# A SwiGLU block's last third by seven products for eight, with its sums made a block earlier

## The chip, the cores and the metric

One core of one Trainium2 chip runs the whole program. The metric is device time in microseconds of one execution, the median of several runs.

## The reference

```python
mask = q_bucket[:, :, :, None] == k_bucket[:, :, None, :]     # buckets: signs of 6 projections
scores = np.where(mask, scale * q @ k.T, -1e9)
attn = softmax(scores) @ v                                    # 4 batches, 8 heads, 768 rows, 64
x = attn.transpose(0, 2, 1, 3).reshape(3072, 512)
g = x @ w_gate                                                # w_gate, w_val: 512 x 1536
silu = g * (1.0 / (1.0 + np.exp(-g)))
out = (silu * (x @ w_val)) @ w_out                            # w_out: 1536 x 512
```

The change is in the second half, from `x` on.

## The kernel before

The attention comes first, a pair of heads at a time. Beside it the weights are read, rounded and split into 36 pieces, which are kept in DRAM (`ram`). `x` is kept transposed: its rows are the 512 features, 128 to a tile.

A product in fp32 is made of three matmuls. Every operand is kept as three parts, high, low and a difference (`[P, 3, 512]` per piece). The products of the first two parts go to one PSUM bank (tile `a`, 16 matmuls for 1024 tokens), those of the third to another (tile `n`, 8 matmuls). The result is `a * (STEP + 1) - n`: ScalarE reads `a` and scales it (L787), VectorE takes `n` off (L794).

The tokens are worked in three blocks of 1024 (the first, second and third block here; `NB` is 3). In each block there are 12 column blocks of 128 of the 1536 features, called U. A U takes one gate piece and one value piece: gate products, Silu (L796), value products, gate times value (L798), and the rounding of the hidden tile into its three parts (L799 on ScalarE, L805 low and L808 difference on VectorE). After three U's whose hidden tiles are ready comes a down part, D: eight chunks of 128 tokens, 9 matmuls each (tile `o`), added to the accumulators by VectorE (L851, L855; ScalarE's L849 in the first part). The last part of a block begins with four part chunks that leave out the last piece, and it stores the output on SP's queue.

The order is written out by hand: the scheduler is off, so every engine runs its instructions in the order in which the loop over `order` issues them. `atoms_of` yields the steps of a U (four: `a` and `n` of gate, `a` and `n` of value) and of a D (one per chunk), and after each of them the loop puts in some steps of other work. In the first block these are the remaining weight pieces (`turns`, paced by `pace`); in the second and third block there is nothing left of them. At a block's end the next block's `x` is loaded from DRAM into three `words` buffers (`load_x`) and split (`split_x`).

Pieces come into SBUF through a ring of six buffers (`bring`, L251, issued on POOL's queue): a load is issued when the piece six places before it has been used. PSUM's eight banks are four tiles of two banks (`two_banks`), taken in turn. All matmuls after the attention have line L748 (`mm`).

Of the kernel before, what the change touches and what calls it, by code (L numbers as in the profile page):

```python
# [8 lines left out]
FP32 = mybir.dt.float32  # L9
# [10 lines left out]
def kernel(  # L20
# [8 lines left out]
    moe_w_out: bass.AP,  # L29
    out: bass.AP,  # L30
):

# [6 lines left out]
    nc = tc.nc  # L41
# [33 lines left out]
    RINGS = (3, 3)  # L75
    ringp = [ctx.enter_context(tc.tile_pool(name="ringp", bufs=RINGS[0]))]
    dram = ctx.enter_context(tc.tile_pool(name="dram", bufs=1, space=bass.MemoryType.DRAM))
    pp = ctx.enter_context(tc.tile_pool(name="pp", bufs=4, space=PSUM))
    ctx.enter_context(tc.manual_schedule())

    def two_banks(name):
        return pp.tile([P, 2, 512], FP32, tag="pp", name=name)

    halves = [slice(half * HQ, (half + 1) * HQ) for half in range(2)]

# [138 lines left out]


    order = []
    for block in range(NB):
        for f in range(NF):
            order.append(("U", block * NF + f))
            if f % NQ == 0 and f:  # L230
                order.append(("D", (block * NF + f) // NQ - 1))
        order.append(("D", (block + 1) * NF // NQ - 1))
    wanted = []
    for kind, n in order:
        if kind == "U":
            wanted += [("g", n), ("v", n)]
        else:
            wanted += [("o", NQ * n + g) for g in range(NQ)]
    held = {}

    def bring(count=1):
        for _ in range(count):
            i = len(held)
            if i == len(wanted):
                return
            what, n = wanted[i]
            at = place[what, n % NF]
            assert progress["kept"] > at, (i, at, progress)
            pool = ringp[2 <= i % sum(RINGS) < 2 + RINGS[1]]
            held[what, n] = t = pool.tile([P, 3, PIECE], FP32R, tag="ring", name="ring")  # L250
            nc.gpsimd.dma_start(t.bitcast(FP32), ram[at].bitcast(FP32))  # L251

    kept_x = {(b, pr): dram.tile([P, S], FP32, tag=f"x{b}_{pr}", name="xram")
              for b in range(1, B) for pr in range(NP)}
# [481 lines left out]
    def gated_block(scope):  # L736
# [7 lines left out]
        rows = [out[b * S : (b + 1) * S, :].rearrange("(p c) m -> p c m", c=NCH) for b in range(B)]  # L744
        NCB = WB // P

        def mm(ps, w, x, start, stop):
            nc.tensor.matmul(ps, w, x, start=start, stop=stop)  # L748

        def up(F, what):  # L750
            b = F // NF
# [24 lines left out]
        def atoms_of(kind, n):  # L776
# [36 lines left out]
                    yield one  # L813
                    yield other
            else:
                b, part = divmod(n, NF // NQ)
                ws = [held["o", NQ * n + j] for j in range(NQ)]
                hs = [hids[NQ * n + j] for j in range(NQ)]
                tiles = {}

                def start(c, js, steps=None):
                    if c not in tiles:
                        tiles[c] = two_banks("o")
                    t = tiles[c]
                    cols = slice(c * P, (c + 1) * P)
                    def first():
                        for j in js:
                            for v in range(2):
                                mm(t[:, 0], hs[j][:, v, cols], ws[j][:, v],
                                   j == 0 and v == 0, j == NQ - 1 and v == 1)  # L830

                    def second():
                        for j in js:
                            mm(t[:, 1], hs[j][:, 2, cols], ws[j][:, 2], j == 0, j == NQ - 1)

                    for go in steps or ("ba" if final and c >= ahead else "ab"):
                        (first if go == "a" else second)()

                def end(c):
                    t = tiles.pop(c)  # L840
                    early = final and c >= ahead
                    if early:
                        nc.vector.tensor_tensor(accs[c], accs[c], t[:, 1], op=ALU.subtract)  # L843
                    if part == 0:
                        if c % 2 == 0:
                            accs[c // 2, "both"] = outp.tile([P, 2, DM], FP32, tag=f"o{c // 2}",
                                                             name="o")
                        accs[c] = accs[c // 2, "both"][:, c % 2]
                        nc.scalar.activation(accs[c], t[:, 0], AF.Copy, scale=STEP + 1)  # L849
                    else:  # L850
                        nc.vector.scalar_tensor_tensor(out=accs[c], in0=t[:, 0],  # L851
                                                       scalar=STEP + 1, in1=accs[c],
                                                       op0=ALU.mult, op1=ALU.add)
                    if not early:
                        nc.vector.tensor_tensor(accs[c], accs[c], t[:, 1], op=ALU.subtract)  # L855
                    if part == NF // NQ - 1:
                        batch, at = divmod(b * NCB + c, NCH)
                        if final and c >= ahead:
                            nc.sync.dma_start(rows[batch][:, at, :], accs[c])
                        elif c % 2:  # L860
                            nc.sync.dma_start(rows[batch][:, at - 1 : at + 1, :], accs[c // 2, "both"])
                    if c == NCB - 1:
                        bring(NQ)

                final = n == NB * NF // NQ - 1
                ahead = 4 if part == NF // NQ - 1 else 0
                for c in range(ahead):
                    yield lambda c=c: start(c, range(NQ - 1))
                def last_diffs(c):
                    tn = two_banks("o")[:, 0]  # L870
                    for j in range(NQ):
                        mm(tn, hs[j][:, 2, c * P : (c + 1) * P], ws[j][:, 2], j == 0, j == NQ - 1)
                    nc.vector.tensor_tensor(accs[c], accs[c], tn, op=ALU.subtract)

                def last(c):
# [3 lines left out]
                    for t, here, queue in ((ts[0], slice(0, DM - P), nc.sync),  # L879
                                           (ts[1], slice(DM - P, DM), nc.scalar)):  # L880
                        t = t[:, 0 : here.stop - here.start]
                        for j in range(NQ):
                            for v in range(2):
                                mm(t, hs[j][:, v, cols], ws[j][:, v, here],
                                   j == 0 and v == 0, j == NQ - 1 and v == 1)
                        nc.vector.scalar_tensor_tensor(out=accs[c][:, here], in0=t,  # L886
                                                       scalar=STEP + 1, in1=accs[c][:, here],
                                                       op0=ALU.mult, op1=ALU.add)
                        queue.dma_start(rows[batch][:, at, here], accs[c][:, here])

                for c in range(NCB):
# [5 lines left out]

                    def chunk(c=c):
                        if c >= ahead:
                            start(c, range(NQ))  # L900
                        else:
                            start(c, [NQ - 1], "ab")
                        end(c)
                    yield chunk

# [22 lines left out]

        raw_x = {}
        mine = turns()  # L930
        for kind, n in order:
            b, f = divmod(n, NF if kind == "U" else NF // NQ)
            changing = b + 1 < NB
            if changing:
                if (kind, f) == ("D", NF // NQ - 2):
                    load_x(b + 1, range(NP // 2))
                elif kind == "U" and f >= NF - 2:
                    assert len(added) == NPIECE
                    splits.extend(split_x(b + 1, f - NF + 2))
                    if f == NF - 1:  # L940
                        load_x(b + 1, range(NP // 2, NP))
            if n == NB * NF // NQ - 1 and kind == "D":
                finish(tails)
            for at, atom in enumerate(atoms_of(kind, n)):
                tail = atom()
                finish(tails)
                if tail:
                    tails.append(tail)
                if changing and kind == "U" and f >= NF - 2 and at:
                    splits.pop(0)()  # L950
                if changing and kind == "D" and f == NF // NQ - 1:
                    if at == 0:
                        more = [split_x(b + 1, pr) for pr in range(NP // 2, NP)]
                        for x in more:
                            x.pop(0)()
                    if at in (7, 10):
                        for x in more:
                            x.pop(0)()
                count[0] += 1
                if left and count[0] in (4, 6, 11):  # L960
                    left.append(left.pop(0)())
# [6 lines left out]
                    pace = (0, 0, 0, 2, 1, 2, 2, 2)  # L968
                else:
                    pace = (0, 0, 1, 0) + (1,) * 8  # L970
                for _ in range(pace[at]):
                    step = next(mine, None)
                    if step:
                        step()

    with ExitStack() as scope:
        gated_block(scope)
# [32 lines left out]
```

## Time and profile before

| | us |
|---|---|
| median of 3 runs | 907.73 (907.3 to 908.71) |
| the profiled execution, its own time | 908.05 |
| its span in the trace | 906.3 |
| TensorE busy (all matmuls) | 901.8 |
| VectorE, ScalarE, GpSimd busy | 665.4, 450.4, 90.6 |

The second block lies between 510.6 and 706.4 us of the span and the third between 706.4 and 902.5 us. Busy time of an engine is the time in which it executed something. TensorE's is close to the span, and its weight loads (PEld) run beside its matmuls. GpSimd (POOL) does little but issue the ring's loads in this half. Of the DMA traffic 114.8 MB go through POOL's queue (q0), and 57.4 MB through SP's (q1).

### The profile page before, as it was taken

Reading aid. Unit: us, or ns where it says so; the run is one execution under the profiler, and the core shown is the slowest. Engines: PE = TensorE matmul, PEld = TensorE weight load, DVE = VectorE, ACT = ScalarE, POOL = GpSimd, SP = SyncE. Lnnn points to the kernel's source line nnn. Section 1 sums busy time; section 2 is a strip of 40 time slices with the busy share of each in tenths; the row PEclk is TensorE's granted clock in tenths of the full one; section 3 lists DMA queues with packets and bytes.
Section 4 is the critical chain, followed back from the end, with each engine's and each line's share of the span. In section 5 each row is a group of like instructions: output and inputs, shape, how many; then the busy total and the mean of one; then the engine's idle time right before and its main releaser. Section 6 shows DMA issues by size and latency. Waiting matters only on the chain.

```text
span 906.3 us, 12438 instructions
## 1 busy us (share of the span) xinstructions
PE 901.8 (100%) x4801; PEld 638.4 (70%) x4801; DVE 665.4 (73%) x782; ACT 450.4 (50%) x604; POOL 90.6 (10%) x187
## 2 busy tenths in 40 slices
PE   9999999999999999999999999999999999999998
PEld 5444444444444588888888888888888888888887
DVE  6779999999988977688786856464658754474746
ACT  6788988788888654551524233331313243413220
POOL 2001100010001210011000000101000100001000
PEclk9999999999999999999999999999999999999999
DMA  7567888877877799685758563534434642525332
GB/s 181 109 145 183 190 203 194 205 203 230 229 195 213 225 358 375 240 294 170 300 173 296 193 249 105 180 134 172 142 140 150 250 149 98 200 70 209 104 140 93
DMA packets 142266, 174.24 MB, mean 192 GB/s; under 512 B 103200, under 2 KB 113408, under 8 KB 142208
## 3 DMA queue, kind: packets, MB, share of 16 engines
q0 software_dynamic: 22240, 114.83, 35.8%
q1 hardware_dynamic: 118560, 57.43, 24.5%
q10 hardware_dynamic: 1408, 1.20, 0.5%
q8 instruction: 38, 0.62, 0.3%
q14 instruction: 20, 0.16, 0.1%
HBM read 133.17 MB, written 39.42 MB: 190 GB/s over the span
## 4 chain that ended last, share of the span: by engine, by line
PE 99%; DVE 0%; DVEq 0%; issue 0%
PE a L748 29%; PE o L748 21%; PE sc L549 17%; PE n L748 14%; PE av L580 14%; PE joint L621 1%; PE joint L441 1%; PE idle L375 0%; PE tps L483 0%; DVE o L843 0%; DVE o L851 0%; DVE o L886 0%; DVEq L1005 0%; DVE kb L369 0%
## 5 line engine op out<-in xcount | busy, mean ns | idle before, releaser
L748 PE MATMUL a<-xparts,ring 128*128 128x512 f32 x1152 | 273.0, 389 | 0.0
L748 PEld LDWEIGHTS a<-xparts,ring 128*128 128x128 f32 x1152 | 216.2, 188 | 45.4 <-issue 0.6
L748 PE MATMUL o<-ring,hid 128*128 128x512 f32 (+1 forms) x870 | 198.2, 388 | 0.0
L748 PEld LDWEIGHTS o<-ring,hid 128*128 128x128 f32 x870 | 162.9, 188 | 33.6
L559 ACT ACTIVATE A<-sc 128x768 f32<-128x768 f32 x192 | 154.0, 815 | 1.6 <-PE sc L549 0.8
L549 PE MATMUL sc<-qT,kT 64*128 64x384 f32 x768 | 153.0, 483 | 0.0
L748 PE MATMUL n<-xparts,ring 128*128 128x512 f32 x576 | 142.2, 389 | 0.0
L580 PE MATMUL av<-A,vraw 128*64 128x386 f32 (+1 forms) x768 | 127.7, 488 | 0.0
L748 PEld LDWEIGHTS n<-xparts,ring 128*128 128x128 f32 x576 | 108.1, 188 | 22.4
L794 DVE TENSOR_TENSOR v<-v,n 128x1024 f32<-128x1024 f32 x36 | 44.0, 1221 | 97.5 <-PE n L748 97.0
L251 POOL DMA_DIRECT2D ring<-ram x108 | 57.0, 530 | 498.7 <-PE n L748 302.4
L580 PEld LDWEIGHTS av<-A,vraw 128*64 128x64 f32 x768 | 53.7, 136 | 73.3 <-issue 62.6
L787 ACT ACTIVATE g<-a 128x1024 f32<-128x1024 f32 x36 | 37.0, 1027 | 128.0 <-PE a L748 126.9
L549 PEld LDWEIGHTS sc<-qT,kT 64*128 64x128 f32 x768 | 68.8, 187 | 39.8 <-issue 35.3
L799 ACT ACTIVATE hid<-v 128x1024 fp32r<-128x1024 f32 x36 | 38.2, 1062 | 111.9 <-DVE v L798 108.2
L796 ACT ACTIVATE g<-g 128x1024 f32<-128x1024 f32 x36 | 38.2, 1061 | 87.9 <-DVE g L794 87.9
L855 DVE TENSOR_TENSOR o<-o 128x512 f32<-128x512 f32 x92 | 62.9, 687 | 19.0 <-ACT o L849 16.6
L794 DVE TENSOR_TENSOR g<-g,n 128x1024 f32<-128x1024 f32 x36 | 43.8, 1217 | 37.5 <-PE n L748 37.5
L549 PE MATMUL sc<-qb,kb 64*128 64x384 bf16 x384 | 63.5, 323 | 0.0
L603 DVE SCALAR_TENSOR_TENSOR both<-A 128x1536 f32<-128x1536 f32 x32 | 55.5, 1734 | 4.5 <-ACT A L559 3.0
L805 DVE SCALAR_TENSOR_TENSOR hid<-hid,v 128x1024 fp32r<-128x1024 f32 (+1 forms) x39 | 44.5, 1141 | 18.8 <-ACT hid L799 18.8
L607 DVE TENSOR_TENSOR both<-both,A 128x1536 f32<-128x1536 f32 x32 | 55.9, 1748 | 1.7
(88 smaller groups left out, 695.5 us busy)
## 6 DMA issues: line engine op xcount, KB each, us to landing
ring<-ram POOLq DMA_DIRECT2D x108, 768.0 KB, 5.6
ram<-stage POOLq DMA_DIRECT2D x22, 768.0 KB, 4.5
ram<-stage SPq DMA_DIRECT2D x14, 768.0 KB
vraw<-in_v_dram SPq DMA_DIRECT2D x16, 384.0 KB
kraw<-in_k_dram SPq DMA_DIRECT2D x60, 96.0 KB
qraw<-in_q_dram SPq DMA_DIRECT2D x60, 96.0 KB
r<-sums SPq DMA_DIRECT2D x28, 192.0 KB
out_dram<-o SPq DMA_DIRECT2D x10, 512.0 KB
```

The lines of the kernel that those rows point to most:

```text
L251: nc.gpsimd.dma_start(t.bitcast(FP32), ram[at].bitcast(FP32))
L549: nc.tensor.matmul(banks_of[u][:, h], x["k", n][rows, ks], x["q", n][rows, qs], start=start, stop=stop)
L559: nc.scalar.activation(weights(u)[:, :, 0:HQ], banks_of.pop(u), AF.Exp, scale=SCALE * (1.0 if units[u][0] else OFF / 2))
L580: nc.tensor.matmul(ps[h * D : (h + 1) * D, 0:width], raws["v", n][:, h, c, :], a[:, h, 0:width], start=c == 0, stop=c == NCH - 1)
L603: nc.vector.scalar_tensor_tensor(out=t, in0=first, scalar=S * EPS / P / 2, in1=now, op0=ALU.add, op1=ALU.add)
L607: nc.vector.tensor_tensor(t, t, now, op=ALU.add)
L748: nc.tensor.matmul(ps, w, x, start=start, stop=stop)
L794: nc.vector.tensor_tensor(two(z), two(z), n_, op=ALU.subtract)
L796: nc.scalar.activation(z, z, AF.Silu)
L799: nc.scalar.activation(h, val, AF.Copy, scale=TOWARD / STEP)
L805: nc.vector.scalar_tensor_tensor(out=l_, in0=h_.bitcast(FP32), scalar=-STEP, in1=v_, op0=ALU.mult, op1=ALU.add)
L855: nc.vector.tensor_tensor(accs[c], accs[c], t[:, 1], op=ALU.subtract)
```

## The change

In the third block two neighbouring column blocks of one weight, with the features cut in two halves of 256 and the tokens in two halves of 512, make a 2 x 2 by 2 x 2 product of quarters. It is done in seven products of quarters (6 matmuls each: two feature tiles, three parts) for eight. A group is such a set of seven: `g` or `v` for each of six pairs. With A the weights and B the tokens, the sums are S1 = A21 + A22, S2 = S1 - A11, S3 = A11 - A21, S4 = A12 - S2, and T1 = B12 - B11, T2 = B22 - T1, T3 = B22 - B12, T4 = B21 - T2.

Results that are used twice are copied: after A11 B11 ScalarE copies the two banks of Y to those of X, and A12 B21 is added to X by TensorE; after S2 T2 has been added to Y, Y is copied to Z; S3 T3 and then A22 T4 are added to Y, S4 B22 to Z. S1 T1 is read out to SBUF (`five`) and added by VectorE to two of the results. Each of the four results is read by ScalarE, and VectorE takes off the second bank (`less`). PSUM's tiles are single banks in this block. The rounding of the hidden tiles of one group is spread over the slots of the next group (`then`, `at_slot`).

The third block's down parts take four pieces for three, so there are three of them, with 12 matmuls per chunk. A group brings four ring pieces: the row, S1 and S2, S3 and S4, and the half of the second row that holds A22.

The sums are made in the second block, where `mine` is replaced by `all_sums`: 12 sets for the weights and 4 for x. Their steps are put in behind the steps of the U's and D's: two, one, two, one in a U, one per chunk in a D. A set loads two raw tiles into `words` buffers (SP), adds on GpSimd, rounds on ScalarE (`high`) and VectorE (`low`, `diff`) and stores to DRAM (SP). At the end of the second block T1 to T3 come back into the places of x's tiles and T4 into the three `words` buffers. B11, B21 and B22 are split from x as before, the last two earlier in the block's last D.

The order in which the engines get the work: TensorE has 3835 matmuls for 3905, VectorE 32 instructions on `made`, ScalarE 16, and POOL's queue now has the sets' additions among the ring's loads.

```diff
-    for block in range(NB):
+    for block in range(NB - 1):
...
+            else:
+                src = sums[what[0], n][:, 0 if what[1:] == "12" else 1]
...
+        def all_sums():
+            count = 2 * NG + 4
+            raws = {0: raw_parts(0)}
+            homes_ = {}
+            def add(i):
+                a, c = raws.pop(i)
+                t = homes_[i] = xparts_p.tile([P, 2, 3, PIECE], FP32, tag=f"x{2 + i % 2}", name="made")
+                tt = nc.gpsimd.tensor_tensor
+                lo, hi = slice(0, PIECE), slice(PIECE, 2 * PIECE)
+                if i < 2 * NG:
+                    tt(a[:, lo], a[:, lo], a[:, hi], op=ALU.add)
+                    tt(c[:, lo], c[:, lo], c[:, hi], op=ALU.add)
+                    k0, k1 = slice(0, HP), slice(HP, PIECE)
+                    s1, s2, s3, s4 = t[:, 0, 1, k0], t[:, 0, 1, k1], t[:, 1, 1, k0], t[:, 1, 1, k1]
+                    tt(s1, c[:, k0], c[:, k1], op=ALU.add)
+                    tt(s3, a[:, k0], c[:, k0], op=ALU.subtract)
+                    tt(s2, s1, a[:, k0], op=ALU.subtract)
+                    tt(s4, a[:, k1], s2, op=ALU.subtract)
...
+            def high(i):
+                t = homes_[i]
+                nc.scalar.activation(r32(t[:, :, 0]), t[:, :, 1], AF.Copy,
+                                     scale=TOWARD if i < 2 * NG else TOWARD / STEP)
...
+            for i in range(count + 1):
+                if i < count:
+                    yield lambda: add(i)
+                if i:
+                    yield lambda: low(i - 1)
+                    yield lambda: diff(i - 1)
+                if i + 1 < count:
+                    yield lambda: raws.update({i + 1: raw_parts(i + 1)})
+                if i < count:
+                    yield lambda: high(i)
...
-                    if at in (7, 10):
+                    if at in ((2, 4) if b == LAST - 1 else (7, 10)):
                         for x in more:
                             x.pop(0)()
+                        if at == 2:
+                            fourth_sum()
...
+                if b == LAST - 1:
+                    if kind == "U" and f < NF - 2 or kind == "D" and f < NF // NQ - 1:
+                        for _ in range((2, 1, 2, 1)[at] if kind == "U" else 1):
+                            step = next(made[0], None)
+                            if step:
+                                step()
+                    continue
...
+            product(Y, "A11", "B11", True, x_copy, lambda: copied(late["X"], Y, 1))
+            at_slot(1)
+            product(V, "S1", "T1", True, lambda: read(five, V), lambda: less(five, V))
+            at_slot(2)
+            product(Y, "S2", "T2", False, z_copy, lambda: copied(late["Z"], Y, 1))
+            bring()
+            at_slot(3)
+            X, Z = late["X"], late["Z"]
+            product(X, "A12", "B21", False, lambda: read(C[0, 0], X), lambda: less(C[0, 0], X))
+            bring()
+            if what == "v":
+                closing(0, 0)()
+            at_slot(4)
+            product(Y, "S3", "T3", False, lambda: read(C[1, 1], Y), lambda: less(C[1, 1], Y))
+            more_(C[1, 1])
+            if what == "g":
+                closing(0, 0)()
+            at_slot(5)
+            product(Z, "S4", "B22", False, lambda: read(C[0, 1], Z), lambda: less(C[0, 1], Z))
+            bring()
+            more_(C[0, 1])
+            closing(1, 1)()
+            at_slot(6)
+            product(Y, "A22", "T4", False, lambda: read(C[1, 0], Y), lambda: less(C[1, 0], Y))
+            bring()
+            if what == "g":
+                closing(0, 1)()
+                then(2, closing(1, 0))
+                return
...
+            then(1, closing(0, 1))
+            then(1, closing(1, 0))
+            then(1, lambda: high(0))
+            then(2, lambda: low(0))
+            then(3, lambda: diff(0))
+            then(3, lambda: high(1))
+            then(4, lambda: low(1))
+            then(5, lambda: diff(1))
```

`closing` is the Silu of a quarter (ScalarE) in a `g` group and gate times value (VectorE) in a `v` group; `more_` adds `five`; here `high`, `low` and `diff` at the end are those of the hidden tiles.

## Prediction, made blind

> **What bounds the kernel now.** I read the chain of work that ended last first, then its pieces in order of time, then the engines' busy time by block, then the DMA rate. The page's chain:
>
> ```profile
> PE 99%; DVE 0%; DVEq 0%; issue 0%
> PE a L748 29%; PE o L748 21%; PE sc L549 17%; PE n L748 14%; PE av L580 14%; PE joint L621 1%; PE joint L441 1%; PE idle L375 0%; PE tps L483 0%; DVE o L843 0%; DVE o L851 0%; DVE o L886 0%; DVEq L1005 0%; DVE kb L369 0%
> ```
>
> TensorE sets the end everywhere, so a matmul removed is worth its full pace, and any wait that PE doesn't have yet is a loss. The pace is in the chain in order of time (start, length, what), at the second block's first column block and first down part:
>
> ```profile
> 510.72 3.63 PE a L748 x16
> 514.35 1.81 PE n L748 x8
> ...
> 554.24 16.32 PE o L748 x72
> ```
>
> 3.63/16 and 16.32/72 are both 0.227 us per matmul (the 389 ns of the groups are overlapped durations). A column block U (two weights, 48 matmuls) is 10.88 us, a down part of 72 is 16.32 us, its chunk of 9 is 2.04 us. By block of 1024 tokens (PE, PEld, DVE, ACT, POOL busy, clock, DMA share, GB/s):
>
> ```profile
> 510.60:706.40 195.80, 195.80 (x866) 162.15 (x864) 118.74 (x127) 58.44 (x60) 18.93 (x36) 1.00 0.46 167
> 706.40:902.50 196.10, 196.10 (x871) 162.66 (x869) 114.30 (x125) 54.74 (x56) 17.38 (x33) 1.00 0.41 146
> ```
>
> In the second block DVE is 61% busy, ACT 30%, DMA 46%: there seems to be room. How fast DMA can go shows in single microseconds where its share is 1:
>
> ```profile
> 341.00:342.00 1.00, 1.00 (x6) 0.84 (x5) 0.97 (x2) 0.33 (x1) 0.00 (x0) 1.00 1.00 418
> 351.00:352.00 1.00, 1.00 (x6) 0.84 (x5) 0.97 (x2) 0.00 (x0) 0.00 (x0) 1.00 1.01 418
> 869.00:870.00 1.00, 1.00 (x6) 0.84 (x5) 0.13 (x1) 0.07 (x1) 0.00 (x0) 1.00 1.03 424
> ```
>
> So about 418 GB/s is full. The prices of the vector work:
>
> ```profile
> L855 DVE TENSOR_TENSOR o<-o 128x512 f32<-128x512 f32 x33 | 22.6, 687 | 8.2 <-ACT o L849 7.4
> ...
> L808 DVE TENSOR_TENSOR hid<-hid 128x1024 fp32r<-128x1024 f32 (+1 forms) x13 | 14.9, 1143 | 0.4
> ...
> L849 ACT ACTIVATE o<-o 128x512 f32<-128x512 f32 x8 | 4.7, 596 | 8.6 <-PE o L748 8.6
> ```
>
> A bank costs DVE 0.69 us or ACT 0.60 us; 128x1024 costs DVE 1.14 us.
>
> **What the Trainium skill says.** *GPSIMD Engine Reference*, section "Performance versus the Vector engine": a GpSimd two-input add takes 4497 ns for 2048 fp32 per partition. POOL runs no such add in this trace; I use the figure. *SBUF — State Buffer*, "Who interferes with whom": a DVE instruction with two SBUF inputs and a GpSimd instruction that reads SBUF exclude each other, and the second to issue waits until the first ends. No row here shows it either. *DMA: Bandwidth & Descriptors*, "Issuing engines are not separate DMA queues": transfers from SP and POOL share the same 16 engines. The trace agrees: with the ring loads of POOL and the stores of SP both running (351 to 352 us) the sum is still 418 GB/s.
>
> **The change, part by part.**
>
> *Removed.* In the third block a pair of column blocks of one weight takes 7 products of 6 matmuls for 48 matmuls: 6 fewer, in 12 groups: 72 x 0.227 = 16.3 us, all on PE's path. The down parts of four pieces for three do the same matmuls (two more short ones in the last chunk, under 0.5 us).
>
> *Added in the second block: sixteen sets of sums.* Each set loads two raw tiles of 0.52 MB (SP), adds 2048 elements per partition on POOL (two sets of x half of that), rounds 128x1024 on ACT (1.06 us), does two 128x1024 on DVE (2.3 us) and stores 1.57 MB (SP). Engine sums: DVE 118.7 + 37 = 155 of 195.8 us, ACT 58 + 17 = 75, POOL 19 + 14 x 4.5 + 2 x 2.2 = 86. None is full, so as busy time this is nothing; it's the order that costs. The sets go out in 79 steps, 6 per U and 8 per down part, so they span ten U, two down parts and three chunks: 10 x 10.88 + 2 x 16.32 + 3 x 2.04 = 147.6 us, five steps (one set) per 9.3 us.
>
> DMA in that stretch: 16 x 2.62 = 42 MB, and the ring's 36 x 0.786 MB per 195.8 us make 21.3 MB more: 63.3 MB in 147.6 us is 429 GB/s, above 418. Even with no gap it takes 152 us, 4 us more.
>
> There will be gaps, as each set waits for the last one. The "words" pool has three buffers and a set holds two, so the second raw tile of set i+1 is loaded only when set i's adds have ended, and on SP it stands behind the store of set i-1 and the first raw tile, and ahead of the store of set i. Let C be the time from one set's adds to the next's. The store of set i-1 is issued some 5 us after its adds (ACT 1.06, DVE 2.3, the rest work queued ahead on DVE). Ring loads take 145 of the 418 GB/s, which leaves 270: store and first tile (2.1 MB) take 7.8 us and are through 12.8 - C after set i's adds. Then the second tile, 1.9 us, about 1 us to land, and the adds that need it, 3.4 us (4.5 less the first 512 elements): C = 12.8 - C + 6.3, C = 9.6 us. The exclusion comes on top. In a U DVE has two-SBUF-input work for 3.5 (hid and gate products) + 2.7 (1.2 sets) = 6.2 of 10.9 us. An add meets it with a chance of 0.57 and then waits half of 1.14 us, 0.33 us; doubled, since DVE slips in again between adds, 0.65, and none in down parts: some 0.4 us for each of five adds, 2 us. Then 2C = 21.1, C = 10.6 us. Bounds: no contention 9.6 (DMA's own limit without gaps is 63.3/42 x 2.62/418 = 9.4), a full DVE instruction ahead of each add 12.4. A gain is excluded: PE has no wait here to lose.
>
> Who waits: behind a late set stand ACT's rounding, behind that the next eviction of `a` (L787), behind that PE's bank. Rounding comes four steps (7.4 us) after the adds' place; the adds end about 10 us after it; ACT may be 6.2 us late before PE wants the bank back (1.8 + 3.6 + 1.8 us, less the 1.03 of the eviction). So about 4 us are spare, once. POOL's ring loads behind late adds have a lead of 17 to 28 us against 5.6 us to land: no cost. Loss in the second block: 15 x (10.6 - 9.3) - 4 = 15 us.
>
> *Block change.* T1 to T4 (6.3 MB) come beside x, output and ring: 17.6 MB in the last 38 us, 463 GB/s, but T4 is wanted only 8 us into the third block, and the outputs behind T2 to T4 on SP hold only accumulators that are next written some 40 us later. The x splits that move to steps 2 and 4 of the last down part are the same four DVE instructions (4.8 us), under four part chunks of 5.4 us; if the x loads are late behind the stores, DVE and then the banks wait. 0, at most 5 us.
>
> *Third block, waits.* A product is 1.36 us, a group 9.52 us. ACT per g group that follows a v group: four bank copies, five reads, three or four Silu at 0.6 and two roundings at 1.06: 9.3 of 9.52 us. DVE there: seven banks at 0.69, two products, two lows, two diffs: 10.8 us. Followed queue by queue (evictions start 0.26 us after PE moves on, as ACT's does after `a` at 868.04 us): `less` of the fourth read of Y is behind low and diff of the last hid and ends about 9.7 us into the group, while the seventh product writes that bank from 9.1: 0.7 us, five times. The last Silu of the g group waits for DVE until about 13 us, and the next group's first bank copy stands behind it on ACT, wanted at 12.9 and done at 14.1: 1.3 us, in the three cases where no down part comes between. Together 7.4 us. On POOL the groups' ring loads have leads of over 9 us; only after a down part of four pieces the third next piece is wanted 5.4 us after its load can start, and a load lands in 5.6: nothing to speak of. Bounds: 3 (DVE catches up while PE waits) and 10.
>
> *End.* The last down part's cover (four chunks x 6 matmuls, 5.4 us) is as long as before, the rounding of the last hid comes from a DVE that is some 1 us later: 1 us (0 to 2).
>
> *Sum:* -16.3 + 15 + 0 + 7.4 + 1 = +7.1 us. The profiled execution (span 906.3, its own time 908.05) is within 0.4 us of the median 907.73; 907.7 + 7.1 = 914.8, say 915 us.
>
> **The rivals.** *The sets keep up (faster).* Everything turns on C: the loss of the second block equals what the third gains (7.9 us) at C = 9.3 + (7.9 + 4)/15 = 10.1 us. If the adds hardly meet DVE and SP's queue has no gap, C is 9.4 to 9.6, the second block loses 0 to 1 us, the third gains 9: about 899 to 900 us. For it: POOL is idle, no engine is above 80%. Against: 429 GB/s asked of 418.
> *The exclusion is full.* Each add and each DVE instruction alternate: C = 12.4, loss 15 x 3.1 - 4 = 42 us, 942 us. For it: the rule as the skill puts it; against: in down parts DVE reads one operand from PSUM and doesn't take part.
> *The sets lose about as much as the third block gains:* within 0.2%.
> *The change doesn't do what it says:* the order of PE shows 70 fewer matmuls, so it does.
>
> **Numbers.** Slower as forecast, 915 (its own range 909.5 to 925): 0.44. Exclusion near full, around 942: 0.15. Same: 0.06. Faster, around 900: 0.35. 0.2% (1.8 us) is about what a measurement of this kernel can tell from no change. The range runs from 896 (no gaps, third-block waits of 3 us) to 938, which leaves out some 0.05 below and 0.12 above.
>
> **What would show it.** Right: in the second block PE gaps at `a`, released by ACT, with ACT waiting at its rounding for POOL, and POOL for a DMA into words; a DMA share near 1; the block some 15 us longer than 195.8. Third block near 187 us, not 179.8, with waits of PE for ACT at `y`. Wrong: GpSimd adds of 512 elements much under or over 1.1 us, DVE's rows unchanged beside them, second block still 196 us (then faster), or over 220 us.

## The result, and the profile after

The changed kernel takes 958.7 us (957.19 to 960.17, 4 runs) against 907.79 for the kernel before: a ratio of 1.056, 95% interval 1.054 to 1.0579. The forecast was 915 with a range of 896 to 938. The sign was right; the size was 44 us short. The trace counts 4731 TensorE instructions for 4801, so the 70 fewer that the change promised are there.

The page of the kernel after, the chain of work that ended last, by engine and by line:

```profile
PE 68%; DVE 9%; DMA 9%; POOL 6%; issue 5%; ACT 2%; SPq 1%; POOLq 0%; DVEq 0%; ACTq 0%
PE sc L600 16%; PE o L799 14%; PE av L631 13%; PE a L799 11%; PE n L799 5%; DMA words<-ram 5%; PE y L799 3%; DMA words<-xram 2%; DMA ring<-ram 1%; PE joint L672 1%; PE x L799 1%; PE joint L492 1%; POOL words L1016 1%; DVE hid L856 1%; DVE made L1040 1%
```

Before, TensorE had 99% of the chain. Now a third of it lies on the vector engines, the DMA and the issue of work, and the names are those of the sets: `words` (raw tiles), `made`. The second and the third block, each up to its end in this kernel (PE, PEld, DVE, ACT, POOL busy, clock, DMA share, GB/s):

```profile
510.57:765.64 255.07, 218.62 (x865) 171.97 (x864) 175.71 (x164) 71.33 (x76) 130.74 (x123) 0.90 0.84 319
765.64:955.17 189.53, 183.32 (x800) 148.67 (x800) 125.10 (x176) 90.14 (x154) 31.84 (x55) 1.00 0.62 225
```

The second block went from 195.8 to 255.1 us (+59.3), the third from 196.3 to 189.5 (-6.8). So the whole loss is in the second block, with the same number of matmuls. PE was idle there for 36.5 us (255.07 less 218.62). It was busy for 22.8 us more than before with the same matmuls (218.62 less 195.80), at a granted clock of 0.90 for 1.00. No engine is full: DVE has 69%, POOL 51%, the DMA 84%. The loss is in a chain, and the chain in order of time shows it. Here are the first two sets of the kernel after, cut from the chain of the window 510 to 545 us (start, length, what):

```profile
516.03 0.33 SPq L913
...
516.45 8.17 DMA words<-ram
...
526.04 1.29 POOL words L1016
...
527.40 0.72 POOL made L1019
...
532.36 1.99 POOL words L1016
```

SP issues an output store (L913) at 516.03, when VectorE has finished the first block's last chunk; only behind it comes the first raw load, which takes 8.2 us. The first set's additions (L1016 on 512 elements 1.29 us, L1019 on 256 elements 0.72) run while DVE is waiting. The second set's L1016 takes 1.99. The timelines of DVE and of POOL a moment later, kernel after (start, length, instruction):

```profile
535.50 1.76 DVE L1048 SCALAR_TENSOR_TENSOR made<-made 128x1024 fp32r<-128x1024 f32 x1
537.19 1.76 DVE L856 SCALAR_TENSOR_TENSOR hid<-hid,v 128x1024 fp32r<-128x1024 f32 x1
538.98 1.65 DVE L859 TENSOR_TENSOR hid<-hid 128x1024 fp32r<-128x1024 f32 x1
540.55 1.21 DVE L845 TENSOR_TENSOR g<-g,n 128x1024 f32<-128x1024 f32 x1
```

```profile
534.41 1.77 POOL L1019 TENSOR_TENSOR made<-words 128x256 f32<-128x256 f32 x1
536.14 1.73 POOL L1020 TENSOR_TENSOR made<-words 128x256 f32<-128x256 f32 x1
537.83 1.72 POOL L1021 TENSOR_TENSOR made<-made,words 128x256 f32<-128x256 f32 x1
```

The two engines go in strict turns with a step of 1.7 us. Neither shows a wait: the wait is inside the duration, 1.76 for 1.22 on DVE and 1.73 for 0.72 on POOL. L845, whose second operand is in PSUM, keeps its 1.21. Over the whole second block (line, tile, shape, count, busy us, mean ns, idle time before and its releaser; kernel after):

```profile
L1015 POOL TENSOR_TENSOR words<-words 128x512 f32<-128x512 f32 x12 | 20.7, 1725 | 42.1 <-DMA words<-ram 42.1
L1019 POOL TENSOR_TENSOR made<-words 128x256 f32<-128x256 f32 x12 | 17.0, 1415 | 0.9
L907 DVE TENSOR_TENSOR o<-o 128x512 f32<-128x512 f32 x35 | 23.8, 686 | 5.8 <-ACT o L901 4.8
L1040 DVE TENSOR_TENSOR made<-made 128x1024 fp32r<-128x1024 f32 x12 | 19.7, 1642 | 27.1 <-ACT made L1034 27.1
L859 DVE TENSOR_TENSOR hid<-hid 128x1024 fp32r<-128x1024 f32 x11 | 18.1, 1643 | 0.4
```

L907 (before: L855) has one operand in PSUM and is unchanged at 686 ns. L859 (before: L808, 1225 ns in this block) has two in SBUF and takes 1643. The six additions of a set of weights sum to 7.8 us (1725 + 1716 + 1415 + 1062 + 981 + 879 ns) where they take 5.4 alone (2 x 1.29 + 4 x 0.72). So 2.4 us of a set's additions are the turns, and 5.4 us are their own length. The waits of the same stretch, kernel after (in total, times, longest):

```profile
ACT made L1034 <- POOL made L1022: 64.7, 11, 11.7
POOL words L1015 <- DMA words<-ram: 42.1, 10, 12.6
POOL made L1027 <- DMA words<-xram: 26.9, 2, 14.4
```

ScalarE waits at its rounding for POOL, and POOL for the raw load: the waits that the forecast named, in its order. What makes the load late is not what the forecast named, as the runs with a fourth buffer show.

The rounding on ScalarE gives the period of the sets. Its row in the kernel after (count, durations, first and last start):

```profile
L1034 ACT ACTIVATE made<-made x16: 1039/1059/1062, 530.3 to 711.5; 128x1024 fp32r<-128x1024 f32 x16
```

(711.5 - 530.3) / 15 = 12.1 us per set. TensorE's order has a place for a set every 9.3 us.

### The profile page after: what moved, and what is told of

Its sections match the earlier page's. It is cut to its first block, busy times and chain, and to the rows that moved or that the text cites. A ratio compares the mean times of both kernels' runs of the same rounds, so it can differ in the third digit from the quotient of the medians.

```text
span 958.4 us, 12866 instructions
## 1 busy us (share of the span) xinstructions
PE 911.5 (95%) x4731; PEld 634.1 (66%) x4731; DVE 732.6 (76%) x871; ACT 498.8 (52%) x718; POOL 217.0 (23%) x295
## 4 chain that ended last, share of the span: by engine, by line
PE 68%; DVE 9%; DMA 9%; POOL 6%; issue 5%; ACT 2%; SPq 1%; POOLq 0%; DVEq 0%; ACTq 0%
PE sc L600 16%; PE o L799 14%; PE av L631 13%; PE a L799 11%; PE n L799 5%; DMA words<-ram 5%; PE y L799 3%; DMA words<-xram 2%; DMA ring<-ram 1%; PE joint L672 1%; PE x L799 1%; PE joint L492 1%; POOL words L1016 1%; DVE hid L856 1%; DVE made L1040 1%
## 5 line engine op out<-in xcount | busy, mean ns | idle before, releaser
L799 PE MATMUL o<-ring,hid 128*128 128x512 f32 (+1 forms) x872 | 217.9, 411 | 31.9 <-ACT g L838 11.2
L799 PE MATMUL a<-xparts,ring 128*128 128x512 f32 x768 | 184.3, 393 | 6.2 <-ACT v L838 5.5
L799 PEld LDWEIGHTS a<-xparts,ring 128*128 128x128 f32 x768 | 145.1, 189 | 38.7 <-ACT v L838 6.4
L799 PE MATMUL n<-xparts,ring 128*128 128x512 f32 x384 | 94.8, 389 | 0.0
L799 PEld LDWEIGHTS n<-xparts,ring 128*128 128x128 f32 x384 | 72.1, 188 | 15.0
L907 DVE TENSOR_TENSOR o<-o 128x512 f32<-128x512 f32 x84 | 57.4, 687 | 26.2 <-PE o L799 16.0
L1034 ACT ACTIVATE made<-made 128x1024 fp32r<-128x1024 f32 x16 | 16.9, 1057 | 85.5 <-POOL made L1022 64.7
L799 PE MATMUL y<-xparts,ring 128*128 128x512 f32 x216 | 55.4, 392 | 4.1 <-ACT x L1227 2.6
L847 ACT ACTIVATE g<-g 128x1024 f32<-128x1024 f32 x24 | 25.4, 1060 | 61.6 <-DVE g L845 61.6
L850 ACT ACTIVATE hid<-v 128x1024 fp32r<-128x1024 f32 x24 | 25.5, 1060 | 57.8 <-DVE v L849 54.1
L838 ACT ACTIVATE g<-a 128x1024 f32<-128x1024 f32 x24 | 24.5, 1019 | 57.6 <-PE a L799 57.1
```

The lines of the kernel that those rows point to most:

```text
L799: nc.tensor.matmul(ps, w, x, start=start, stop=stop, **more)
L838: nc.scalar.activation(two(z), ops[what][2], AF.Copy, scale=STEP + 1)
L847: nc.scalar.activation(z, z, AF.Silu)
L850: nc.scalar.activation(h, val, AF.Copy, scale=TOWARD / STEP)
L1034: nc.scalar.activation(r32(t[:, :, 0]), t[:, :, 1], AF.Copy, scale=TOWARD if i < 2 * NG else TOWARD / STEP)
```

## The experiments

All times are against the kernel before, run on the same chip (907.37 to 907.76 us there). "Second block" is the time from its first matmul to the first matmul of the third block in the profiled execution. Where an edit adds lines, the line numbers of that kernel are a few higher than in the kernel after.

### No sets at all

```diff
         def all_sums():
+            return
+            yield
```

The third block loads pieces of `ram` of the same sizes in place of the sums.

> Leaves out the making of the sums (no raw loads, adds, roundings or stores in the second block); the third block loads stored weight pieces in place of the sums, so its results are others and its traffic the same. All theories: the second block is back at 196 us up to its last down part, the third stays at 189 to 190 us as in the changed kernel, so 901 to 907 us in all; the 5.7 us that the last down part of the second block grew by stay if T1 to T4's loads cause them, and go if the late sets do. A third block above 192 us would mean that the sets' lateness had helped it.

Measured: 905.32 us (904.23 to 907.7), ratio 0.9975 (0.9966 to 0.9984). The third block takes 188.4 us, 7.9 less than before. The second takes 201.7, 5.9 more than before, all of it in its last down part (22.18 for 16.32). The end of that part, in the chain in order of time of this kernel:

```profile
695.90 2.35 DVE xparts L345 x2
...
699.58 2.27 DVE xparts L350 x2
...
703.22 6.78 PE o L799 x27
710.00 1.54 issue
711.54 1.62 PE y L799 x6
```

The x splits (L345, L350), moved to the third and fifth step of that part, now stand on the chain ahead of the evictions of `o`. And the third block's first `y` waits 1.54 us after the last matmul of `o`: it starts right after DVE has read the last bank of the old pool (DVE's last L907 starts at 710.8 and takes 0.69), so the single banks seem to be handed over only then. Before, the next `a` followed the last `o` with no such wait. 905.3 us is therefore what this idea gives if its sums cost nothing: 0.25% less than before, and 53.4 us of the second block (255.1 less 201.7) go with the sets.

### No sets, and the splits where they were

The kernel above with the splits after the eighth and eleventh step again, and the loads of T4 behind the first of them.

```diff
-                    if at in ((2, 4) if b == LAST - 1 else (7, 10)):
+                    if at in (7, 10):
...
-                        if at == 2:
+                        if at == 7 and b == LAST - 1:
```

> As the run without sums (making of sums left out, stored pieces loaded in their place), but with the splits of x in the last down part put back to steps 7 and 10, and T4's loads behind step 7. If the moved splits cost the 5.9 us of that down part, it goes back to 16.3 us, and 899 to 902 us are left. If the third block's first matmul waits for the last evictions of all banks, which now come later, 3 to 5 us appear there and the total stays at 903 to 906 us.

Measured: 907.48 us (906.2 to 909.49), ratio 0.9995 (0.9986 to 1.0004). The second block is 201.4 us, the last down part 21.85, of which 5.3 us are one wait between the last `o` and the first `y`. The time lies above both branches. The second had the mechanism and put the wait at 3 to 5 us. So the splits cost about the same in either place: early they hold up evictions, late they hold up the third block. The early place is better by 2 us.

### Additions cut to 8 columns

```diff
+                nc.gpsimd.memset(t[:, :, 1], 0.5)
-                lo, hi = slice(0, PIECE), slice(PIECE, 2 * PIECE)
+                lo, hi = slice(0, 8), slice(PIECE, PIECE + 8)
...
-                    k0, k1 = slice(0, HP), slice(HP, PIECE)
+                    k0, k1 = slice(0, 8), slice(HP, HP + 8)
```

The sums are not computed; raw loads, roundings and stores stay.

> GpSimd's additions are cut to 8 columns each, and the tile is filled by a write that reads nothing; loads, roundings, VectorE's two steps and stores stay (the sums are meaningless). If the additions and their exclusion with VectorE are the main part, a set takes under 9.3 us and the second block 200 to 212 us: 905 to 918 us. If DMA bandwidth is (63 MB asked in 148 us), nothing is relieved: over 940 us.

Measured: 933.34 us (931.47 to 934.63), ratio 1.0288 (1.027 to 1.0305). The second block falls from 255.1 to 227.1: the additions are worth 28 us, their length and the turns together. The time lies between the two branches, so neither tells the whole.

### POOL as busy, but only writing

The kernel above with three fills of the tile in place of one.

```diff
+                for _ in range(3):
+                    nc.gpsimd.memset(t[:, :, 1], 0.5)
```

> As the run without additions, but GpSimd writes the tile three times, so that it is busy for about 5.3 us a set, as long as the additions alone take beside nothing (2 x 1.28 + 4 x 0.72 us), and reads nothing. If the exclusion with VectorE is what the additions cost, this stays within 4 us of the run without additions: 932 to 938 us. If their length in the chain of waits is, most of the 25 us comes back: 945 to 958 us.

Measured: 932.61 us (930.59 to 932.91), ratio 1.0264 (1.0244 to 1.0284), second block 227.5. From the groups of that block, kernel with three fills:

```profile
L1014 POOL MEMSET made<- 128x1024 f32 x48 | 45.9, 955 | 43.4 <-DMA sums_ram<-made 34.5 <-DVE g L845 2.8 <-DVE v L845 2.1
L1042 DVE TENSOR_TENSOR made<-made 128x1024 fp32r<-128x1024 f32 x12 | 14.7, 1221 | 14.1 <-ACT made L1036 14.0
L859 DVE TENSOR_TENSOR hid<-hid 128x1024 fp32r<-128x1024 f32 x11 | 13.5, 1231 | 0.4
```

With the small additions POOL works about 5 us per set here, as long as the full additions take alone, and the block is no longer than with one fill. DVE's rows are at 1221 and 1231 ns, so a GpSimd that only writes doesn't slow VectorE. The run doesn't show that the 28 us are the turns alone. The fills need no raw tile, so they run while POOL would wait for one: its waits for the raw tiles of the weights are 39.7 us in the kernel with one fill and 21.2 here, 18.5 of the 23 us that the two more fills of 12 sets take. The additions need the raw tiles and can't be moved into that wait. How much of the 28 us is their length behind the load, and how much the turns, is not separated.

### Raw tiles loaded once

```diff
+        raw_kept = []
+
         def raw_parts(i):
+            if raw_kept:
+                return raw_kept
...
+                raw_kept.extend(tiles)
                 return tiles
```

All sets work on the first set's raw tiles; the rest stays.

> The two raw tiles are loaded once and used for all sixteen sets (so the sums are others); additions, roundings and stores stay. If the wait for the raw loads on SP behind the stores is the main part, 912 to 925 us. If the exclusion of GpSimd and VectorE is (adds of 7.8 us a set, VectorE's two-operand instructions 1.5 us), it stays over 935 us. If bandwidth is, the traffic is 47 MB in 148 us, below full: 910 to 920 us.

Measured: 945.58 us (943.52 to 948.9), ratio 1.0421 (1.0398 to 1.0444); second block 239.4, 15.7 less than with the loads. The loads aren't the main part, by the branches set out ahead: the time stays over 935 us.

### Both

Raw tiles loaded once and additions of 8 columns; roundings and stores stay.

> Both relieved: raw tiles loaded once, additions cut to 8 columns (the sums are meaningless); roundings, VectorE's two steps and stores stay. If additions and raw loads are two separate shares, nothing but the last down part's 6 us is left in the second block: 196 + 6 us, so 905 to 910 us. If the stores and the roundings themselves cost (traffic, ScalarE and VectorE out of place), 915 to 925 us.

Measured: 914.02 us (913.25 to 914.88), ratio 1.0067 (1.0047 to 1.0088); second block 208.8. The rounding row of this kernel:

```profile
L1040 ACT ACTIVATE made<-made x16: 1041/1056/1065, 527.2 to 667.3; 128x1024 fp32r<-128x1024 f32 x16
```

(667.3 - 527.2) / 15 = 9.34 us: the sets now go at TensorE's pace. Together the two edits take 46.3 us off the block, apart 28.0 and 15.7, so the two shares nearly add. More than this can't come back, since the order of TensorE now sets the pace. The time lies between the two branches, nearer the second. Sixteen roundings and 25 MB of stores by themselves cost some 7 us (208.8 less 201.7). By the count of the table below, 5 of them are the late start.

### A fourth raw buffer

One raw tile of every second set has a buffer of its own, so that no second raw tile waits for the additions of the set before.

```diff
-            tiles = [wordp.tile([P, PIECE, 2], I32, tag="words", name="words") for _ in range(2)]
+            tiles = [(rawp if i % 2 and e else wordp).tile([P, PIECE, 2], I32, tag="words", name="words")
+                     for e in range(2)]
```

> A fourth buffer for the raw tiles, so that both tiles of the next set can be loaded while this set is added; nothing is left out. The recorded prediction's chain (second raw tile waits for the adds) would shrink to under 10 us a set: 925 to 935 us. If the wait is the first tile's, which stands behind the store on SP, little changes: 948 to 958 us.

Measured: 959.82 us (958.83 to 959.93), ratio 1.0572 (1.0556 to 1.0588); second block 256.5. No gain, and the time is 2 us above the second branch: the number of buffers isn't what makes the load late. The forecast's link from set to set, the second raw tile that waits for the additions, is not the one that holds.

### A fourth buffer, and the raw loads ahead of the store

```diff
                     yield lambda: add(i)
+                if i + 1 < count:
+                    yield lambda: raws.update({i + 1: raw_parts(i + 1)})
                 if i:
                     yield lambda: low(i - 1)
                     yield lambda: diff(i - 1)
-                if i + 1 < count:
-                    yield lambda: raws.update({i + 1: raw_parts(i + 1)})
```

> A fourth raw buffer, and in the sets' order the two raw loads of the next set are issued ahead of the low, difference and store of the last set, so on SP no raw load stands behind a store that waits for VectorE. Everything is computed as in the changed kernel. Theory (a third of the second block's loss is that the raw loads are issued late, behind the store, and GpSimd then waits for them): GpSimd's waits for the words buffers go, the second block falls from 255 to about 239 us, as when the raw tiles were kept, and the time to 942 to 947 us. Rival (it is the bytes of the raw loads on the DMA engines, not their place on the queue): the second block stays at 252 to 257 us and the time at 956 to 961.

Measured: 949.82 us (947.9 to 953.86), ratio 1.0469 (1.0439 to 1.05); second block 244.8. Between the two branches: 10 us of the 16 come back. The waits of POOL in the second block of this kernel tell why not all:

```profile
POOL made L1022 <- DMA sums_ram<-made: 26.1, 6, 8.0
POOL made L1030 <- DMA sums_ram<-made: 13.3, 1, 13.3
POOL words L1018 <- DMA words<-ram: 12.6, 1, 12.6
```

The waits for raw tiles are gone but for the first set's. In their place POOL waits for a store to have read its `made` tile: there are two of these tiles, so the store of set i-2 must be through before the additions of set i can write. So the place of the loads on SP was 10 us of the 16. That the rest is the DMA that loads, stores and ring share is argued, not shown. The new order was run only with the fourth buffer, which alone gives nothing.

### The same without the additions

Raw loads ahead of the stores with the fourth buffer, and additions of 8 columns.

> The raw loads ahead of the stores with a fourth buffer, and the additions cut to 8 columns with one fill of the tile in their place (the sums are not computed); raw loads, roundings and stores stay. Theory (with the additions gone what remains is the late place of the loads): the second block falls from the 227 us of the kernel without additions to about 209 to 212 and the time to 914 to 918, as with raw tiles kept. Rival (bytes on the DMA engines): the second block stays at 224 to 228 us and the time at 930 to 934.

Measured: 924.83 us (922.37 to 925.46), ratio 1.0183 (1.0164 to 1.0203); second block 219.2, against 227.1 with the loads behind the stores and 208.8 with no loads. Again in the middle: 7.9 us go with the place of the loads and 10.4 with the loads as such.

### No stores

```diff
-                    nc.sync.dma_start(sums["gv"[i % 2], i // 2], t)
+                    if i == 0:
+                        nc.sync.dma_start(sums["gv"[i % 2], i // 2], t)
```

The same for the sums of x; the third block loads pieces of `ram`.

> Leaves out the stores of the sums, all but the first set of weights and of x; the third block loads pieces of the ring's store in their place, same sizes. Additions, roundings and raw loads are as in the changed kernel. Theory (the raw loads wait behind the stores): the loads now land some 5 us earlier, GpSimd's waits for them go, and the second block falls by 16 to 20 us, to 235 to 239; the time is about 940 to 944. Rival (additions against VectorE set the pace, the loads come late only because the additions are late): the second block stays above 250 and the time above 953.

Measured: 946.96 us (942.77 to 948.89), ratio 1.0425 (1.0389 to 1.046); second block 242.3. A drop of 12.8 us where the theory had 16 to 20: near it, and far from the rival. Taking the stores away, taking the loads away and changing their order each give 10 to 16 us. They are probably three handles on one thing, SP's queue and the DMA behind it; no run takes two of them together with the additions kept.

### The first set's loads earlier

```diff
+                    if at == 4 and b == LAST - 2:
+                        early.extend(raw_parts(0))
...
         def raw_parts(i):
+            if i == 0 and early:
+                return early
```

> Everything is computed as in the changed kernel; only the first set's two raw loads are issued earlier, at the fifth chunk of the first block's last down part, ahead of the output stores on SP (one of them into a spare buffer), so that they have landed when the second block begins. In the changed kernel ScalarE rounds the first set at 530 us, about 12 us behind its place in the order, since the loads are issued 6 us into the block and land 8 us later. Theory (the sets are one chain of 12 us each and TensorE is held to it, so a start that is late by 12 us costs nearly all of that once): the first rounding moves to 518 to 521 us, the second block falls from 255 to 244 to 248 us and the time from 959 to 948 to 952. Rival (the time is set by what the DMA engines and VectorE can do in the block, so that an early first set only waits later): the block stays at 253 to 257 us and the time at 957 to 961.

Measured: 950.01 us (949.63 to 950.26), ratio 1.0463 (1.0446 to 1.0481); second block 247.2. The rounding row of this kernel:

```profile
L1039 ACT ACTIVATE made<-made x16: 1040/1060/1065, 519.4 to 702.5; 128x1024 fp32r<-128x1024 f32 x16
```

The first rounding comes 10 us earlier in the block (9.7 us from its start for 19.7), the period is still (702.5 - 519.4) / 15 = 12.2 us, and the block is 7.9 us shorter: as the theory had it, the late start was paid once and nearly whole.

### The additions on VectorE

```diff
-                tt = nc.gpsimd.tensor_tensor
+                tt = nc.vector.tensor_tensor
```

> The additions are issued on VectorE, nothing is left out. They take it 3.0 us a set by its rows (2 x 0.69 + 4 x 0.41 us), in all 44 us more, 199 to 202 of 196 us in the second block. If the exclusion is the cost, VectorE alone is faster than VectorE beside GpSimd: 930 to 948 us. If VectorE's load is, it gets slower: over 960 us.

Measured: 1024.27 us (1022.29 to 1024.67), ratio 1.1274 (1.1252 to 1.1296); second block 320.3. That is over 960 us, as the second branch had it, but by more than VectorE's load explains: the additions' rows on VectorE sum to 45 us, as expected, and the block grew by 65 over the kernel after. The largest wait of DVE in that block:

```profile
DVE words L1015 <- DMA words<-ram: 54.4, 11, 10.8
```

With four more rows of this kind VectorE waits for raw tiles for some 100 us in all, and every eviction of TensorE's banks stands behind that wait. The run can't tell the exclusion from the load; it shows what the load's wait costs on an engine that TensorE needs.

## Why the prediction was wrong in size

The step that failed is the period C of the sets: put at 10.6 us, measured at 12.1. With it fell the start of the first set, for which the forecast had 4 us to spare and which came 8.1 us beyond its spare. The form of the sum, 15 x (C - 9.3) and a start, holds. With C from the rounding rows, and for the start how far the first rounding lies behind its place (5.4 us into the block, 6.2 us to spare by the forecast's count):

| kernel | first rounding, us into the block | C | 15 x (C - 9.3) + start | block less 201.7 |
|---|---|---|---|---|
| after | 19.7 | 12.1 | 41.7 + 8.1 = 49.8 | 53.4 |
| first loads early | 9.7 | 12.2 | 43.5 - 1.9 = 41.6 | 45.5 |
| loads first | 19.7 | 11.5 | 33.6 + 8.1 = 41.7 | 43.1 |
| no stores | 19.9 | 11.1 | 26.9 + 8.3 = 35.2 | 40.6 |
| raw tiles once | 19.7 | 11.2 | 27.8 + 8.1 = 35.9 | 37.7 |
| no additions | 16.7 | 10.6 | 18.9 + 5.1 = 24.0 | 25.4 |
| both | 16.6 | 9.3 | 0.6 + 5.0 = 5.6 | 7.1 |
| fourth buffer | 19.9 | 12.2 | 43.9 + 8.3 = 52.2 | 54.8 |
| loads first, no additions | 16.6 | 9.8 | 7.9 + 5.0 = 12.9 | 17.5 |

1.4 to 5.4 us remain unaccounted for in each row. 15 C is the time from the first rounding to the last, so the sum is no more than how late the last rounding is. That it fits shows that TensorE is held to the sets; it doesn't test what sets C. For the kernel after, C is 22 us of the 44 that were missing, the start 12 and the block change 6. The terms:

- **C, the main failure: 12.1 for 10.6, some 22 us.** The bound of 12.4 for full exclusion was in the text with a chance of 0.15, and that rival (942 us) was nearer the truth, but by luck: it had the additions lengthened by a whole instruction of VectorE each (5.7 us a set), and they were lengthened by 2.4. Three numbers inside C were too low. The additions alone take 5.4 us, not 4.5: the figure for 2048 elements in one instruction was spread over six small ones. A set's additions with what stands between them take 8.0 us from first to last, not 6.5 (mean of the 12 sets of weights in the trace): the estimate of 0.4 us per addition took POOL's start as a chance meeting, while the timelines show stretches in which the engines are locked in turns (from set to set 5.5 to 10.4 us). And the store is issued 6.7 us after the additions end (mean, 3.7 to 11.7), not 5; its `low` and `diff` stand in the queue of a DVE that the same turns slow, though no run shows how much of the 1.7 us that is. The mechanism was wrong too: the prediction took the second raw tile's buffer for the link from set to set, and the fourth buffer did nothing. The main link is the raw load behind the store on SP (10.3 us when it is taken away), and then the `made` tile behind its store.
- **The start, 12 us.** The forecast counted 4 us to spare once, and had no term for when the first load is issued. In fact the first raw loads stand on SP behind the output stores of the block before, so the first rounding is 8.1 us beyond its spare. The front of a chain needs its own line: where is its first load issued, and what does that wait for?
- **The block change, 0 (at most 5): measured 5.9.** The splits stand among the evictions, as the text feared for late x loads; it didn't need late loads. And it had no term for the change of PSUM's banks, 1.5 us.
- **DMA.** The forecast asked 429 of 418 GB/s. As the sets stretched, the block ran at 319 GB/s on average, so the ceiling did not bind over the whole block. Still the DMA mattered, as the time that loads behind stores take: 7.0 to 11.3 us from issue to landing in the chain of the kernel after. Without the additions the block is nearer the ceiling (DMA share and GB/s are the last two numbers). A single microsecond of the kernel after moves more than 418 (second line), but its share is over 1, and 479/1.14 is 420, so it doesn't show the ceiling passed:

```profile
510.51:737.58 227.07, 203.89 (x866) 163.66 (x864) 158.47 (x164) 71.72 (x76) 68.71 (x139) 0.98 0.94 359
...
620.00:621.00 1.00, 1.00 (x7) 0.81 (x6) 0.00 (x0) 0.00 (x0) 1.00 (x3) 1.00 1.14 479
```

- **The third block: right, in part by luck.** -16.3 + 7.4 + 1 = -7.9; the kernel without sets measured -7.9, the kernel after -6.8. By part it was less good, and the misses cancel: the fourth read of Y cost 0.25 us for 0.7, the bank copy behind the Silu 1.02 for 1.3 (three times, as said), and ring loads, taken for nothing, cost 1.3 and 2.3 us at two down parts of the kernel after. These sum to 7.9 us for 7.4. The copy in the chain of the kernel after:

```profile
796.55 0.70 DVE g L1236
...
797.82 0.59 ACT x L1227
798.45 1.65 PE y L799 x6
```

`y` starts when ScalarE has copied Y's banks away, and ScalarE stood behind a Silu that waited for DVE.

- **The Trainium skill.** *SBUF — State Buffer*, section "Who interferes with whom", is borne out in the main: two-SBUF-input work is delayed (1225 to 1643 ns), one-SBUF-input work is not (686), and fills that only write don't delay it (1231). By the recorded lengths the wait isn't quite for a whole instruction: the step of 1.7 us is less than 1.22 + 0.72 = 1.94. *GPSIMD Engine Reference*, "Performance versus the Vector engine", gives 4497 ns for 2048 elements; the runs show 1.29 us for 512 and 0.72 for 256, so 5.4 us for the same elements in small pieces.

**What stays open.** The clock. TensorE is busy for 22.8 us more in the second block at a granted clock of 0.90; without additions and loads the clock is 0.98. No run separates the clock from the waits that go with it. Not all of it goes with the sets: in the last down part of the kernel after 36 matmuls of the chain take 10.2 us for 8.2, but the kernel without sets has the same there (10.35 us, behind a wait for L907 of 1.95 us, at a granted clock of 0.61 from 699.6 to 704 us). Open too is how the 28 us of the additions divide between their length and the turns. Moving the additions off GpSimd without putting them on VectorE, and issuing the raw loads on another queue than the stores, weren't tried.

## What to carry to other kernels

Work put "beside" a bound engine is not priced by busy shares but by its own chain: write down the period of one unit (load, compute, round, store, buffer free) with every queue it stands in, and the start of the first unit, and compare it with the pace of the host loop. GpSimd arithmetic that reads SBUF beside a VectorE with two-SBUF-input work took turns with it here in the stretches in which both had such work: a set's additions took 5.5 to 10.4 us from first to last. Chance meetings at 0.4 us each were too low a price. And measure the ceiling first: with its sums for free this idea was worth 0.25%.

## What the runs showed that was not expected

- In the locked turns one step is 1.7 us, less than the 1.22 + 0.72 of the two instructions alone, and in the rows shown the wait is in a longer instruction on both engines, not in idle time.
- Three fills of 955 ns per set on GpSimd for one leave the block as it is (227.5 us for 227.1): they run while GpSimd would wait for raw tiles.
- The kernels in which TensorE stalls more in the second block also have a lower granted clock there: 1.00 before, 0.98 without additions and loads, 0.92 with the first loads early, 0.90 with the sets. In the kernel after it was 0.50 in the microseconds at 569, 572 and 575 us, after a stretch in which TensorE stood idle (563 and 566 us).
- A raw load of 0.5 MB behind a 1.5 MB store lands 7.0 to 11.3 us after its issue, where the chain shows it (8.2 in the first set, behind an output store).
